# Float32 feature matmuls of 128 tokens split into two of 64 on halves of TensorE's columns

## The chip, the core and the metric

The kernel runs on one core of a Trainium2 chip. The metric is the device time of one execution in microseconds (us), from the first to the last work of the core; lower is better. TensorE does matrix products in two instructions, a weight load (LDWEIGHTS, written PEld in the profile) that puts the stationary operand (`lhsT`) into the array and a MATMUL (written PE) that streams the moving operand (`rhs`) through it into PSUM. VectorE is DVE, ScalarE is ACT, GpSimd is POOL and SyncE, which issues most DMAs, is SP.

## What is computed

Three layers run one after the other on 4 sequences of 1088 tokens. The first is a linear attention with 4 heads of 32 dimensions, the second a gated feed-forward layer of width 1024 whose input is mixed with the token before, the third a gated MLP that mixes along the sequence with a 1088 x 1088 matrix. The change lies in the first, in `phi`:

```python
def phi(x):
    a = np.einsum('rd,bhsd->bhsr', S1, x)
    b = np.einsum('rd,bhsd->bhsr', S2, x)
    return np.einsum('bhsi,bhsj->bhsij', a, b).reshape(*x.shape[:-1], r * r)
q_p, k_p = (phi(q), phi(k))
kv = np.einsum('bhsf,bhsd->bhfd', k_p, v)
z = np.sum(k_p, axis=2)
num = np.einsum('bhsf,bhfd->bhsd', q_p, kv)
den = np.einsum('bhsf,bhf->bhs', q_p, z)[..., None] + 1e-06
return (num / den).astype(np.float32)
```

With r = 8 each token and head gets 8 values `a` and 8 values `b`, that is 16 per head and 64 for the four heads, and their outer product of 64 features per head.

## The kernel before, in words

Queries and keys lie in SBUF with their 128 dimensions (4 heads x 32) on the partitions and the tokens along the free axis. A sequence of 1088 tokens is cut into three chunks of 384, 384 and 320 tokens (`CH`, line 22), so there are 12 chunks of queries and 12 of keys. `features` (line 204) handles one chunk: for each of its three blocks of 128 tokens (the last block of a 320-token chunk overlaps the one before) it issues one float32 matmul at line 208. Its weights are the 128 tokens (128 dimensions x 128 tokens), its moving operand is `Sbd`, a 128 x 128 matrix. The first 64 columns of `Sbd` are S1 and S2 laid out block by block for the four heads; the last 64 are zeros, since the mask `mk` that it is multiplied with (line 849) has ones only in its first four of eight columns. So a matmul writes 128 tokens on the PSUM partitions and 128 columns, of which the first 64 are wanted; the next block's matmul starts 64 columns further on and writes over the zeros. Each float32 matmul of the program becomes two passes on TensorE, each of one weight load and one MATMUL; 24 chunks with three blocks are 72 matmuls of the program and 144 passes in the trace.

After the three blocks ScalarE copies half of the 64 columns, or all of them, out of PSUM (line 211 or 216, through `copy` at line 134), and VectorE or GpSimd makes the outer product (line 219). For keys (`k_feat`, line 224) the features are summed with the values in `k_sum` (matmuls at line 239, mask at line 244). For queries (`q_feat`, line 249) they are transposed on TensorE (`q_turn`, line 260), multiplied with the sums (`q_num`, line 276, with the division at lines 280 to 282), and transposed back (`q_out`, line 294).

The feed-forward layer works on groups of 128 hidden features: `up` and `down` (lines 354 and 398) use three products of split operands in the faster float32r format (`mm3`, line 128, all under line 131) or one float32 product (line 406). The third layer, `spatial` and `group` (lines 548 and 694), fills the second half of the time with float32r products under line 131.

The order is set in three ways. The program first does the keys of sequence 0, the first chunk of queries, and the keys of sequence 1 (lines 892 to 931). Then one loop over the 96 groups of the feed-forward layer (line 1011) calls whatever `plan` has put down for a group: chunk j of queries at group `QS[j]`, its transposes, products and output two or three groups later, the keys of sequences 2 and 3 some groups ahead of their first query (lines 946 to 962). `behind` (line 896) holds single steps back until a named instruction has been issued. Last, the framework orders each engine's instructions by a simulated timeline (line 1157), so that the six passes of one chunk can stand apart on TensorE with other matmuls between them.

Of the kernel before, what the change touches and what calls it, by code (L numbers as in the profile page):

```python
# [21 lines left out]
CH = ((0, 384), (384, 384), (768, 320))  # L22
# [62 lines left out]
def attn_moe_gmlp(ctx: ExitStack, tc: tile.TileContext, qT, kT, va, st, wk, wv, wr, win, wout,  # L85
                  wT, wtail, btail, mu, ident, msk, out):
    nc = tc.nc
    TE, VE, SE, GE = nc.tensor, nc.vector, nc.scalar, nc.gpsimd
# [7 lines left out]
    def sb(tag, shape, dt=F32):  # L96
        uid[0] += 1
        return pool.tile(shape, dt, tag=tag, bufs=1, name=f"{tag}_{uid[0]}")

    def bank(i):  # L100
        uid[0] += 1
        return pp.tile([128, 512], F32, tag=f"p{i}", bufs=1, name=f"p{i}_{uid[0]}")
# [3 lines left out]
    def rot(*tags):  # L106
        i = count.get(tags, 0)
        count[tags] = i + 1
        return tags[i % len(tags)]

    def m(i):
        return f"m{i}"
# [20 lines left out]
    def copy(dst, src):  # L133
        return SE.activation(out=dst, in_=src, func=AF.Copy)  # L134
# [25 lines left out]
    def flat(r):  # L160
        return r.rearrange("p a b -> p (a b)")
# [14 lines left out]
    def cut(c, t, o=0):  # L176
        a = CH[c][1] - 128 if t == 2 else 128 * t
        return slice(o + a, o + a + 128)
# [25 lines left out]
    def features(src, c, dst, pb=4, eng=None, early=False):  # L204
        wide = bank(pb)
        ab = wide[:, :192].rearrange("p (t h r) -> p t h r", t=3, h=NH)
        for t in range(3):
            TE.matmul(wide[:, 64 * t:64 * t + 128], lhsT=src[:, cut(c, t, CH[c][0])], rhs=Sbd, start=True, stop=True)  # L208
        if eng is None:
            bs = sb(rot("bs0", "bs1"), [128, 3, NH, 8])  # L210
            copy(bs, ab[:, :, :, 8:16])
            a_ = ab[:, :, :, 0:8].rearrange("p t h i -> p (t h) i")
            b_ = bs.rearrange("p t h j -> p (t h) j")
        else:
            sab = sb(m(2 + c) if early else "sab", [128, 3, NH, 16])
            copy(sab, ab)
            a_ = sab[:, :, :, 0:8].rearrange("p t h i -> p (t h) i")
            b_ = sab[:, :, :, 8:16].rearrange("p t h j -> p (t h) j")
        outer[0] = (eng or VE).tensor_tensor(
            out=dst.rearrange("p t (h i j) -> p (t h) i j", h=NH, i=8),  # L220
            in0=a_.unsqueeze(3).to_broadcast([128, 3 * NH, 8, 8]),
            in1=b_.unsqueeze(2).to_broadcast([128, 3 * NH, 8, 8]), op=ALU.mult)

    def k_feat(b, c, pb=4, eng=None):
        kp = kps[b, c] = sb((KB1 if b == 1 else ("n0H", "n0L", "n1H"))[c], [128, 3, 256])
        features(k_s[b], c, kp, pb, GE if 3 * b + c in KP else eng, eng is not None)
# [22 lines left out]
    def q_feat(i):  # L249
        qp = qst[i] = sb("n1L", [128, 3, 256])  # L250
        features(q_s[i // 3], i % 3, qp, 4, GE if i in QP else None)
# [599 lines left out]
    Sbd = flat(Sb)  # L851
# [309 lines left out]
```

## Time and profile before

| what | value |
|---|---|
| median of 3 runs | 451.74 us |
| lowest and highest run | 451.67 and 452.97 us |
| span of the profiled execution, first to last instruction | 450.7 us |
| TensorE MATMUL busy | 440.8 us, 98% of the span, 2691 instructions |
| TensorE weight loads busy | 420.4 us, 93% |
| VectorE, ScalarE, GpSimd busy | 297.5, 270.4, 223.2 us |
| MATMULs of line 208 | 144, first start at 4.7 us, last at 130.2 us |

The profile gives the span of one execution from its first to its last instruction. It has no time of its own for that execution beside the span; the median run is 1.04 us longer than the span, and that is taken for what lies around it. MATMULs are pipelined: each record lasts from its issue to a modelled end, and the next one starts long before that end, so a MATMUL's duration isn't what it costs in a stream. The cost in a stream is the distance from one start, or end, to the next, which the chain of work that ended last shows: there each instruction counts only from the end of the one before it. "x6" after a piece is the number of instructions in it.

### The profile page before, as it was taken

What the parts mean: (1) busy time and instruction counts of PE and PEld (TensorE: products, weight loads), DVE (VectorE), ACT (ScalarE), POOL (GpSimd) and SP (SyncE); (2) the same over time, 40 slices, a digit from 0 to 9 for tenths busy, and PEclk for the clock granted to TensorE, in tenths of its full rate; (3) what the DMA queues carried; (4) which work ended last, traced back from release to release, by engine and by line L of the source; (5) the groups of instructions that cost most, each with busy time, mean ns of one, the idle gap of its engine ahead of it and who ended that gap; (6) DMA issues with size and microseconds to landing.
All of it is one profiled execution on the core that took longest, in us unless ns stands there. A gap on an engine that the chain in (4) does not pass through costs nothing.

```text
span 450.7 us, 7621 instructions
## 1 busy us (share of the span) xinstructions
PE 440.8 (98%) x2691; PEld 420.4 (93%) x2691; DVE 297.5 (66%) x531; ACT 270.4 (60%) x629; POOL 223.2 (50%) x271
## 2 busy tenths in 40 slices
PE   8899999999999999999999999999999999999997
PEld 7897989989998988899999999999999999999996
DVE  5995777779864986566587797862755951734513
ACT  2595888998977898767446664334545434533322
POOL 2166477496744585868222426544435534335220
PEclk9999999999999999999999999999999999999999
DMA  7981100011100030033238422313022232010001
GB/s 232 369 297 49 51 0 2 2 52 54 27 2 0 22 120 19 19 87 113 59 117 256 131 63 93 118 54 110 15 85 93 72 110 69 19 41 25 0 2 49
DMA packets 30950, 34.92 MB, mean 77 GB/s; under 512 B 2816, under 2 KB 26432, under 8 KB 30912
## 3 DMA queue, kind: packets, MB, share of 16 engines
q1 hardware_dynamic: 30768, 34.43, 23.8%
q8 instruction: 21, 0.34, 0.3%
q14 instruction: 17, 0.14, 0.1%
q10 hardware_dynamic: 144, 0.01, 0.0%
HBM read 25.91 MB, written 8.52 MB: 76 GB/s over the span
## 4 chain that ended last, share of the span: by engine, by line
PE 84%; DVE 6%; DMA 3%; ACT 3%; POOL 1%; issue 1%; SPq 1%; ACTq 0%; DVEq 0%
PE p L131 67%; PE p L406 5%; PE p L276 3%; PE p L239 2%; PE p L208 2%; DMA w<-in_wk_dram 1%; PE p L260 1%; PE p L722 1%; PE p L721 1%; DMA st<-in_wT_dram 1%; DVE w L148 1%; DVE w L147 1%; PE p L294 1%; ACT m L362 1%; DVE mx L319 1%
## 5 line engine op out<-in xcount | busy, mean ns | idle before, releaser
L131 PE MATMUL p<-m,k 128*128 128x384 f32 (+1 forms) x288 | 65.5, 349 | 0.0
L131 PE MATMUL p<-w,k 128*128 128x384 f32 (+1 forms) x360 | 63.8, 323 | 0.0
L131 PEld LDWEIGHTS p<-w,k 128*128 128x128 f32 x360 | 59.2, 188 | 0.3
L621 DVE TENSOR_TENSOR m<-p,m 128x384 f32<-128x384 f32 (+2 forms) x37 | 18.6, 520 | 57.0 <-PE p L722 56.1
L134 ACT ACTIVATE m<-m 128x384 fp32r<-128x384 f32 (+2 forms) x49 | 24.6, 502 | 45.9 <-DVE m L735 25.6
L131 PEld LDWEIGHTS p<-m,k 128*128 128x128 f32 x288 | 48.2, 189 | 4.1
L137 POOL TENSOR_TENSOR k<-VR,k 128x512 fp32r<-128x512 f32 x25 | 34.0, 1364 | 33.4 <-ACT k L134 28.6
L362 ACT ACTIVATE m<-p 128x384 f32<-128x384 f32 (+1 forms) x96 | 43.1, 468 | 8.2 <-PE p L131 6.4
L137 DVE TENSOR_TENSOR m<-m,m 128x384 fp32r<-128x384 f32 (+1 forms) x48 | 34.3, 715 | 11.2 <-ACT m L134 8.8
L131 PE MATMUL p<-w,n1H 128*128 128x384 f32 (+1 forms) x192 | 41.1, 326 | 0.0
L365 POOL TENSOR_TENSOR m<-m 128x384 f32<-128x384 f32 (+1 forms) x35 | 30.0, 859 | 21.5 <-ACT m L362 21.0
L137 DVE TENSOR_TENSOR w<-m,w 128x384 fp32r<-128x384 f32 (+1 forms) x35 | 26.0, 746 | 15.4 <-POOL m L365 11.4
L131 PE MATMUL p<-w,n1L 128*128 128x384 f32 (+1 forms) x168 | 34.8, 324 | 0.9 <-POOL n1L L137 0.9
L134 ACT ACTIVATE m<-p 128x384 f32<-128x384 f32 (+1 forms) x36 | 17.1, 482 | 30.0 <-PE p L131 21.7
L137 POOL TENSOR_TENSOR n1H<-VR,n1H 128x512 fp32r<-128x512 f32 x12 | 15.5, 1293 | 37.1 <-ACT n1H L134 26.4
L406 PE MATMUL p<-w,wvT 128*128 128x384 f32 (+1 forms) x86 | 33.4, 470 | 0.0
L131 PEld LDWEIGHTS p<-w,n1H 128*128 128x128 f32 x192 | 32.6, 188 | 0.5
L500 POOL TENSOR_SCALAR rs<-mv 128x1 f32<-128x1 f32 x34 | 8.8, 260 | 43.3 <-DVE mv L499 42.4
L131 PEld LDWEIGHTS p<-w,n1L 128*128 128x128 f32 x168 | 28.5, 188 | 1.4 <-POOL n1L L137 1.2
L504 DVE TENSOR_SCALAR VR<-VR,mv,rs 128x512 f32<-128x512 f32 x24 | 20.5, 855 | 12.6 <-POOL rs L501 12.3
L134 ACT ACTIVATE k<-VR 128x512 fp32r<-128x512 f32 x25 | 15.7, 630 | 21.4 <-PE p L131 17.1
L131 PE MATMUL p<-w,xs1H 128*128 128x384 f32 (+1 forms) x90 | 26.9, 338 | 0.0
(288 smaller groups left out, 1212.6 us busy)
## 6 DMA issues: line engine op xcount, KB each, us to landing
vd<-VR SPq DMA_DIRECT2D x24, 256.0 KB, 2.0
VR<-vd SPq DMA_DIRECT2D x24, 256.0 KB, 2.9
st<-in_wT_dram SPq DMA_DIRECT2D x16, 192.0 KB, 2.4
w<-in_kT_dram SPq DMA_DIRECT2D x8, 192.0 KB, 4.4
w<-in_qT_dram SPq DMA_DIRECT2D x8, 192.0 KB, 4.0
VR<-in_wT_dram SPq DMA_DIRECT2D x8, 192.0 KB, 2.6
out_dram<-m SPq DMA_DIRECT2D x8, 192.0 KB, 2.1
m<-in_wT_dram SPq DMA_DIRECT2D x8, 192.0 KB, 4.5
```

The costliest lines, as they stand in the source:

```text
L131: TE.matmul(out_ap, lhsT=l, rhs=r, start=first and n == 0, stop=last and n == 2, skip_group_check=skip)
L134: return SE.activation(out=dst, in_=src, func=AF.Copy)
L137: return eng.tensor_tensor(out=L, in0=src, in1=H.bitcast(F32), op=ALU.subtract)
L208: TE.matmul(wide[:, 64 * t:64 * t + 128], lhsT=src[:, cut(c, t, CH[c][0])], rhs=Sbd, start=True, stop=True)
L239: TE.matmul(kv[:, w * g:w * g + w], lhsT=kp, rhs=vt if wide else vt[:, VP * g:VP * g + VP], start=(t == 0), stop=(t == NT - 1))
L276: nd_pe[0] = TE.matmul(o.rearrange("p h c -> p (h c)"), lhsT=qt[g][:, cut(c, t)], rhs=kb[:, g], start=not wide or g == 0, stop=not wide or ...
L362: SE.activation(out=r, in_=hk, func=AF.Relu)
L365: anchor[2] = GE.tensor_tensor(out=sq, in0=r, in1=r, op=ALU.mult)
L406: TE.matmul(vvs[i], lhsT=wvT[:, f // 2], rhs=hls.pop(g), start=f == 0, stop=f == NF - 1)
L500: GE.tensor_scalar(out=rs, in0=mv[:, 1:2], scalar1=1e-6, scalar2=None, op0=ALU.add)
L504: VE.tensor_scalar(out=v, in0=r, scalar1=mv[:, 0:1], scalar2=rs, op0=ALU.subtract, op1=ALU.mult)
L621: return eng.tensor_tensor(out=o, in0=a, in1=b_, op=op)
```

## The change

Each matmul at line 208 becomes two. The weights of each are 64 of the 128 tokens, the moving operand is the first 64 columns of `Sbd`, and the result goes to PSUM partitions 0 to 63 for the first half and 64 to 127 for the second, into the 64 wanted columns only. A matmul with 64 columns of weights and an output that starts at partition 0 or 64 is placed on one half of the array's columns, over all 128 of its rows. Nothing else is touched: the copies, the outer products, the DMAs and the order of the calls are as they were. The zeros are no longer written, nor read by anything.

```diff
         for t in range(3):
-            TE.matmul(wide[:, 64 * t:64 * t + 128], lhsT=src[:, cut(c, t, CH[c][0])], rhs=Sbd, start=True, stop=True)
+            a = cut(c, t, CH[c][0]).start
+            for o in (0, 64):
+                TE.matmul(wide[o:o + 64, 64 * t:64 * t + 64], lhsT=src[:, a + o:a + o + 64], rhs=Sbd[:, :64], start=True, stop=True)
```

## Rows read from the trace of the kernel before

**Rows 1.** The page: busy time of each engine, and the granted TensorE clock in 40 slices.
```profile
PE 440.8 (98%) x2691; PEld 420.4 (93%) x2691; DVE 297.5 (66%) x531; ACT 270.4 (60%) x629; POOL 223.2 (50%) x271
...
PEclk9999999999999999999999999999999999999999
```

**Rows 2.** Stretches: start:end, length, each engine's busy us (x instructions), clock, DMA share, GB/s.
```profile
core 0: us, PE busy (x) PEld busy (x) DVE busy (x) ACT busy (x) POOL busy (x), PEclk, DMA share, GB/s
4.00:25.00 21.00, 19.14 (x153) 18.29 (x153) 17.05 (x31) 9.38 (x23) 1.51 (x2) 1.00 1.00 344
25.00:45.00 20.00, 18.91 (x128) 16.59 (x128) 15.12 (x28) 14.77 (x38) 14.87 (x13) 1.00 0.45 149
45.00:131.00 86.00, 85.33 (x542) 77.97 (x541) 67.23 (x116) 74.54 (x185) 55.99 (x60) 1.00 0.08 25
```

**Rows 3.** Line 208 alone in the same stretches: busy us (x passes), clock, DMA share, GB/s.
```profile
core 0: us, PE busy (x) PEld busy (x), PEclk, DMA share, GB/s
4.00:25.00 21.00, 6.37 (x48) 6.12 (x48) 1.00 1.00 344
25.00:45.00 20.00, 4.26 (x30) 3.88 (x30) 1.00 0.45 149
45.00:131.00 86.00, 9.94 (x66) 9.43 (x66) 1.00 0.08 25
```

**Rows 4.** The page: shares of the span on the chain that ended last.
```profile
PE 84%; DVE 6%; DMA 3%; ACT 3%; POOL 1%; issue 1%; SPq 1%; ACTq 0%; DVEq 0%
PE p L131 67%; PE p L406 5%; PE p L276 3%; PE p L239 2%; PE p L208 2%; DMA w<-in_wk_dram 1%; PE p L260 1%; PE p L722 1%; PE p L721 1%; DMA st<-in_wT_dram 1%; DVE w L148 1%; DVE w L147 1%; PE p L294 1%; ACT m L362 1%; DVE mx L319 1%
```

**Rows 5.** The same chain in order of time: start, length (us), what, how many.
```profile
4.48 6.67 DMA w<-in_wk_dram
...
17.42 0.57 DVE VR L282
...
33.75 0.67 PE p L208 x6
...
35.27 0.65 PE p L406 x2
...
45.61 1.29 PE p L276 x12
...
57.28 0.83 POOL mx L318
...
58.14 1.85 DVE mx L319
...
89.43 0.22 PE p L208 x2
...
129.82 0.67 PE p L208 x6
```

**Rows 6.** What TensorE waited for, first from 4 to 45 us, then from 45 to 160 us.
```profile
PE p L276 <- DVE kb L244: 1.1, 1, 1.1
PE p L294 <- DVE VR L282: 0.7, 2, 0.4
...
PE p L131 <- DVE de L281: 0.7, 1, 0.7
PE p L260 <- POOL n1L L219: 0.3, 1, 0.3
```

**Rows 7.** The timeline of PE from 33 to 47 us: start, length, instruction, tiles, shape.
```profile
33.58 0.83 PE L208 MATMUL p<-Sbd,w 128*128 128x128 f32 x6
...
35.11 0.81 PE L406 MATMUL p<-w,wvT 128*128 128x384 f32 x2
...
45.45 1.45 PE L276 MATMUL p<-kb,VR 128*128 128x66 f32 x12
```

**Rows 8.** Line 208, all its passes: duration ns min/median/max, first and last start, shape.
```profile
L208 PEld LDWEIGHTS p<-Sbd,w x144: 186/192/330, 4.4 to 130.1; 128*128 128x128 f32 x144
L208 PE MATMUL p<-Sbd,w x144: 270/275/377, 4.7 to 130.2; 128*128 128x128 f32 x144
```

**Rows 9.** Line 208 from 7.40 to 7.46 us, the one pass there, behind an idle TensorE.
```profile
L208 PEld LDWEIGHTS p<-Sbd,w x1: 186/186/186, 7.4 to 7.4; 128*128 128x128 f32 x1
L208 PE MATMUL p<-Sbd,w x1: 377/377/377, 7.4 to 7.4; 128*128 128x128 f32 x1
its engine sat idle before it (us, times) until:
  DMA w<-in_qT_dram: 1.2, 2
```

## The prediction

> **What bounds the kernel now.** I read the page first. TensorE is busy for 98% of the span at a granted clock of full speed in every slice, that is at the higher of its two levels, 2.4 GHz; no other engine passes 66% [rows 1]. But a share over the span hides stages, so the stretches come next, with line 208 alone in each. From 45 to 131 us TensorE is busy for 85.3 of 86.0 us, and 66 of the 144 passes of line 208 lie there; 30 lie between 25 and 45 us, and 48 before 25 us, where the DMA engines are full (share 1.00) [rows 2, 3]. Third is the chain of work that ended last: 84% of it is TensorE, and line 208 has 2% [rows 4]. Followed in time, it holds 17 pieces of line 208 from 33.75 to 129.82 us, nine of six passes, one of four and seven of two: 72 passes, exactly half of the 144, or 12 of the 24 chunks [rows 5]. The other half is beside something. Up to 25 us the chain runs over the load of `wk` and then VectorE, down to the division at 17.42 us [rows 5], and TensorE waits for VectorE for 1.1 and 0.7 us in all [rows 6]: the eight chunks (48 passes) before 25 us are covered by that. Of the five between 25 and 45 us three stand on the chain; of the eleven after 45 us nine do, and the other two lie beside GpSimd and VectorE around 57 us [rows 5]. The last view is the waits after 45 us: TensorE waits for 0.7 us and 0.3 us, no more [rows 6]. So on these 72 passes, each nanosecond more or less on TensorE is a nanosecond of the end.
>
> **What a pass costs now.** A MATMUL's record is 275 ns long [rows 8] but they overlap; on the chain six passes take 0.67 us, so 112 ns each, and 224 ns for one matmul of the program [rows 5]. Two other rows tell what makes the 112. A float32 pass with 384 moving columns takes 0.65/2 = 325 ns [rows 5, 7], so each further column costs (325 - 112)/256 = 0.83 ns and the part that doesn't depend on columns is 112 - 128 x 0.83 = 5.5 ns. A pass with only 66 moving columns, but the same 128 columns of weights, still takes 1.29/12 = 107.5 ns [rows 5, 7]; its columns would need 60 ns. So the weight load, or the issue of the pair, has a floor of its own at 107.5 ns, and in line 208 that floor and the moving columns weigh the same. The zeros in the moving operand are thus nearly free: dropping them alone would save 4.5 ns a pass.
>
> **What the change adds and removes.** 72 matmuls of the program become 144, so 144 passes become 288: weights half as wide, moving columns halved. No DMA is issued and no wait is added; the copy that reads the bank waits for the last of twelve passes in place of six, and behind it nothing else is queued that TensorE needs at once (the next matmuls are of the feed-forward layer). I cost that copy's delay at nothing while TensorE has such work; without it the delay is the lengthening of one burst, below.
>
> *One pass.* The moving columns give 64 x 0.83 + 5.5 = 59 ns. The weight floor is seen at one width only. Bounds: if it falls with the width, 107.5/2 = 54 ns; if it is issue and doesn't fall, 107.5 ns. I take 59, since a 66-column pass is 4.5 ns cheaper than a 128-column one and a weight load's record of 192 ns [rows 8] is long enough to be streaming. One after the other, twelve passes take 708 ns where six took 672: +36 ns a chunk, 12 x 36 = **+0.4 us**. At 107.5 ns they take 1290 ns: +618 ns a chunk, +7.4 us.
>
> *Two halves side by side.* The halves use different columns of the array and write different partitions. If the second half's first pass runs beside the first half's second pass, and so on down the burst, two passes go in each slot of 59 ns: 6 x 59 = 354 ns, -318 ns a chunk, **-3.8 us**. No row shows two MATMULs of this kernel side by side: every piece above is in single file. I take zero as the nearest row, and keep -3.8 us as the bound.
>
> *The change of shape.* The passes of before have weights of 128 x 128, one after another [rows 7]. After the change TensorE goes from full width to half and back around each of the 17 pieces on the chain, 34 times. No row shows such a step. Below: nothing, since weight loads now run ahead of the MATMUL before them whatever its line. Middle: the new weights can't be loaded ahead, as in the pass behind an idle TensorE at 7.44 us, whose MATMUL starts with its load and takes 377 ns where the median is 275, 102 ns more [rows 8, 9]. That is 102 ns on the way back and, with half the columns, 51 on the way in: 153 ns a piece, 17 x 153 = **+2.6 us**. Above: TensorE also empties first, so that 275 - 112 = 163 ns of each last pass is bare; 34 x 163 = 5.5 us more, +8.1 us. I take the middle, because it is the one row in which a load wasn't hidden. The 12 chunks off the chain would take 12 x 36 ns and at most 12 x 153 ns, 2.3 us; these lie under the load of `wk` and VectorE early on, and if that cover were gone these 2.3 us came on top.
>
> The sum: +0.4 + 2.6 = **+3.0 us** on a span of 450.7 us, that is 453.7 us; with the 1.04 us by which the median run exceeds the span, **454.7 us** against 451.74, 0.7% slower.
>
> A rule that bears on the last term: the Trainium skill, page "TensorEngine Tiling (Array Packing)", section "Key Properties", says that changing the tiling mode, not just the tile, drains TensorE. By that rule the step is at its upper bound, and the time would be 460.2 us; no run here shows it yet.
>
> **Rivals.**
>
> *Side by side, and the change of shape is free.* -3.8 us, 447.9 us. For it: the two halves share neither columns nor PSUM partitions, and loads already run under MATMULs here. Against it: the two halves read their weights in turn, and a floor of 107.5 ns for a pass with few columns says that loads are a stream of their own; if they stay in single file at 54 ns each, twelve take 648 ns and nothing is won. The place is the 17 pieces; it decides as soon as the overlap saves a chunk more than 2.6/12 us = 217 ns. The same page, same section, says that different tiles can load weights and multiply in parallel; no row here shows that.
>
> *Side by side, with the loads bare at each step.* -3.8 + 2.6 = -1.2 us, 450.5 us: within 0.3% of before, which is about what a measurement of this kernel can tell from no change (1.36 us).
>
> *In single file and the step free*, so the change of shape and the parallel halves both don't exist: +0.4 us, 452.1 us. This is also what is seen if the halves are run as ordinary full-width matmuls with idle columns.
>
> *TensorE empties at each step.* +0.4 + 8.1 = 460.2 us in single file, 456.0 us side by side. For it: every one of the 17 pieces stands alone among matmuls of full width. Against it: in the present trace a line never costs extra behind another one, but these all have one shape.
>
> *The order changes.* The framework places 12 matmuls where 6 stood and may part them more often; seven pieces of two passes are there already. Each further piece on the chain costs 153 ns by the middle price, ten of them 1.5 us.
>
> **How the numbers follow.** Forecast (single file, loads bare) 0.33; side by side and free 0.20; side by side with bare loads 0.17, a third of that beyond the 0.3%; single file and free 0.15; emptying 0.10; another order or a floor of issue 0.05. Faster by over 0.3%: 0.20 + 0.05 + 0.02 = 0.27. Within: 0.12 + 0.15 + 0.02 = 0.29. Slower: 0.33 + 0.10 + 0.01 = 0.44. The range goes from the side-by-side case less a little, 447.4 us, to 459.0 us, which leaves out emptying in single file and a floor of issue for all passes. The forecast's own range is 453 to 457 us, by further pieces or a dearer step.
>
> **What would show it.** Right: 288 passes under the changed line, about 59 ns from one to the next in a burst, and the next matmul of full width some 100 ns later than behind a pass of before. Side by side: bursts of twelve that take about 0.35 us on the chain, where six took 0.67. Emptying: gaps of 160 ns or more ahead of and behind each burst. Wrong altogether: pieces of unchanged total length, or a difference that lies outside 25 to 131 us.

## The result and the profile after

The changed kernel takes 457.01 us (median of 4 runs, 456.36 to 457.19) where the kernel before takes 452.29 us (4 runs): a ratio of 1.0097, 95% interval 1.0080 to 1.0113. It is slower, by 4.7 us; the span of the profiled execution went from 450.7 to 455.4 us, also 4.7 us.

All passes of the feature matmuls (now line 210; the lines below it have moved by two), durations in ns as min/median/max, and the longest entry of what ended the idle time ahead of them:
```profile
L210 PEld LDWEIGHTS p<-Sbd,w x288: 132/138/227, 4.7 to 139.4; 128*64 128x64 f32 x144
L210 PE MATMUL p<-Sbd,w x288: 222/222/320, 4.7 to 139.5; 128*64 128x64 f32 x144
...
its engine sat idle before it (us, times) until:
  issue: 5.3, 22
```

These answer to [rows 8]: 288 passes of half the width. New is the last line: 22 times the record of the weight loads (PEld) is empty just ahead of such a pass, for 5.3 us in all, and the cause is "issue", that is nothing that the profile shows: no semaphore, no other engine. The same view of the kernel before names a DMA (1.2 us, twice) and ScalarE (0.3 us, once) there, and no "issue". The record of the MATMULs has no such hole, since theirs overlap.

One chunk kept together, the timeline of PE and of its weight loads from 55.7 to 57.1 us (start, length, instruction, count):
```profile
55.69 0.51 PE L131 MATMUL p<-w,xs1H 128*128 128x384 f32 x2
56.13 0.57 PE L210 MATMUL p<-Sbd,w 128*64 128x64 f32 x12
56.62 0.80 PE L131 MATMUL p<-m,k 128*128 128x384 f32 x3
...
56.12 0.43 PEld L210 LDWEIGHTS p<-Sbd,w 128*64 128x64 f32 x12 [0.25 <-issue]
```
And the first 40 ns of it, line 210 from 56.10 to 56.14 us:
```profile
L210 PE MATMUL p<-Sbd,w x2: 270/270/270, 56.1 to 56.1; 128*64 128x64 f32 x2
```

Read in four steps. **Side by side:** twelve passes have their first and last start within 0.57 - 0.22 = 0.35 us (five steps of 58 ns and the 0.05 us of the next step), and two of them start in the first 40 ns, while a half that runs alone, further down, has its two passes 0.33 - 0.22 = 0.11 us apart. So the halves do run beside each other: six slots of 58 ns in place of six passes of 112. **Way in:** the MATMUL ahead started at 55.86 us (the second of the two at 55.69, each 0.17 us); behind it one of full width would have started 0.17 us later, this one starts at 56.13, after 0.27: 0.09 us in which nothing starts. I read them as TensorE emptying; the trace shows the gap and not its cause. Its first two passes last 270 ns where the median is 222: 0.05 us of bare weight load. **Way out:** the last pass starts at 56.70 - 0.22 = 56.48 us (56.474 unrounded), the next matmul of full width at 56.62 (56.625), after 0.15 where a slot is 0.058: 0.09 us of emptying; and that one lasts 441 ns where 338 is usual, 0.10 us of bare load. **Together** 0.09 + 0.05 + 0.09 + 0.10, some 0.35 us, once for each piece, however many passes it has. (With some narrower matmuls behind it the same reckoning gives 0.30.) From the end of the MATMUL ahead (56.20) to the end of the first one behind (57.42 less two more of 0.175) are 0.87 us; less that one's own 0.175 the piece cost 0.70 us. Six passes of before cost 0.67 [rows 5]. A chunk that stays together is thus nearly even. One that is broken up is not:
```profile
89.57 0.38 PE L262 MATMUL p<-idn,n1L 128*128 128x128 f32 x2
89.88 0.33 PE L210 MATMUL p<-Sbd,w 128*64 128x64 f32 x2
90.14 0.79 PE L131 MATMUL p<-m,k 128*128 128x384 f32 x3
```
By the same reckoning (90.93 - 0.35 - 89.95 - 0.175) this single half of a block, without a partner, costs 0.46 us. Two passes of before, which did a whole block, cost 0.22 [rows 5].

The framework made many such pieces. From 27 us on there are 29 (before: 21): seven of 12 passes, three of ten, one of eight, seven of six, three of four and eight of two. An odd half runs alone, so these 192 passes take 114 slots in place of 96. The sum is 29 x 0.35 + 114 x 0.058 = 16.7 us against 96 x 0.112 = 10.8 us. Reckoned from the trace for each of the 29 pieces by itself, as for the two above, it is 16.1 us against 10.7, the waits left out: **+5.4 us on TensorE**. What TensorE waited for from 27 to 215 us (in total, times, longest):
```profile
PE p L131 <- DVE w L137: 0.8, 1, 0.8
PE p L131 <- DVE de L283: 0.8, 1, 0.8
PE p L131 <- ACT w L396: 0.7, 1, 0.7
PE p L262 <- DVE n1L L221: 0.2, 1, 0.2
```
That is 2.5 us; the same view of the kernel before has 3.3 us (0.9 and 0.3 for GpSimd, 0.7 for ScalarE, 0.7, 0.4 and 0.3 for VectorE). A slower TensorE waits 0.8 us less: 5.4 - 0.8 = 4.6 us after 27 us. That looks like the whole of the 4.7 us, but it isn't quite, for something is lost earlier as well. The first division on VectorE, which starts at 17.42 us in [rows 5], starts here at
```profile
18.23 0.56 DVE L284 TENSOR_TENSOR VR<-p,de 128x384 f32<-128x384 f32 x1
```
0.8 us later, and what TensorE does behind it is as late. Early and late together come to 5.4 us, 0.7 more than the span shows; the view of the waits leaves out the shortest, and these 0.7 us stay unaccounted for.

### The profile page after: what moved, and what is told of

It is laid out like the page before. It is cut to its first block, busy times and chain, and to the rows that moved or that the text cites. A ratio compares the mean times of both kernels' runs of the same rounds, so it can differ in the third digit from the quotient of the medians.

```text
span 455.4 us, 7909 instructions
## 1 busy us (share of the span) xinstructions
PE 445.4 (98%) x2835; PEld 417.3 (92%) x2835; DVE 296.7 (65%) x531; ACT 270.5 (59%) x629; POOL 221.9 (49%) x271
## 4 chain that ended last, share of the span: by engine, by line
PE 46%; DVE 3%; ACT 2%; DMA 2%; issue 1%; POOL 0%; ACTq 0%; SPq 0%
PE p L131 43%; PE p L724 1%; PE p L723 1%; DMA vd<-VR 1%; DVE m L623 1%; DMA VR<-vd 1%; DMA st<-in_wT_dram 1%; DVE VR L623 1%; ACT m L134 1%; DVE VR L506 0%; DVE m L137 0%; DVE xs0L L137 0%; DVE bn L500 0%; ACT T L134 0%; POOL rs L503 0%
## 5 line engine op out<-in xcount | busy, mean ns | idle before, releaser
L137 DVE TENSOR_TENSOR w<-m,w 128x384 fp32r<-128x384 f32 (+1 forms) x35 | 24.6, 708 | 16.9 <-ACT w L396 6.1
```

Of the source, the lines that this page charges most:

```text
L137: return eng.tensor_tensor(out=L, in0=src, in1=H.bitcast(F32), op=ALU.subtract)
```

## Experiments

Kernels that ran on the same chip share the runs of the kernel before (medians 452.0 to 452.4 us). Ratios are to it, with the 95% interval; times of kernels from different chips are best compared by their distance to it.

### Pieces kept together, and its control

In the changed kernel the first matmul of a chunk stays where it is, and the other five are queued right behind it with priority; the control does the same to the three of the kernel before. Both have 20 pieces, 16 of them after 27 us.
```diff
+        lead = None
         for t in range(3):
             a = cut(c, t, CH[c][0]).start
             for o in (0, 64):
-                TE.matmul(...)
+                with ExitStack() as es:
+                    if lead is not None:
+                        es.enter_context(tc.issue_after(lead.ins))
+                        es.enter_context(tc.high_priority())
+                    x = TE.matmul(...)
+                    lead = lead or x
```


> The changed kernel, but the twelve passes of a chunk are kept together on TensorE (20 pieces in place of 33). Theory A (the loss is a fixed price of each change of shape, about 0.35 us for a piece however many passes it has, while the passes themselves run two at a time in 58 ns): from 27 us on there are 16 pieces in place of 29, so 13 x 0.35 = 4.5 us and some 1.0 us of half matmuls that found no partner go away; of these 5.5 us a fifth was beside other work, so about 4.4 us: 452 to 453 us, level with the kernel before. Theory B (the halves themselves are slow, or the new order of the other matmuls costs the time): still 456 to 457 us.

> The kernel before, with the three matmuls of a chunk kept together in the same way (20 pieces in place of 25), no change of shape. Theory A: at full width a piece has no price, so nothing changes: 451.5 to 453 us. If keeping them together is itself worth or costs something, it shows here and must be taken off the run above.

Measured: 454.46 us (1.0048, 1.0032 to 1.0065), and the control 452.75 us (1.0014, 1.0002 to 1.0027). The breaking up is over half of the loss: 457.0 to 454.5 us. Theory A had 452 to 453 us, and the miss is the last 1.7 us above the control. TensorE's own sum is 16 x 0.35 + 96 x 0.058 = 11.1 us, +0.4 us on before, so it isn't there. Its waits from 27 to 215 us in this run add up to 4.0 us, 0.7 more than before and 1.2 more than in the control (2.8), among them new ones on operands that other engines make for the feed-forward layer:
```profile
PE p L131 <- ACT xrH L134: 0.8, 2, 0.4
PE p L131 <- DVE x L418: 0.5, 1, 0.5
PE p L131 <- POOL xrL L137: 0.5, 1, 0.5
```
0.4 + 1.2 = 1.6 us of the 1.8 us by which the spans of this run and the control differ (452.4 and 450.6). So theory A holds for the pieces, and the rest is waits. The framework lays the order of the other engines' work anew for every program; that these waits come from that order is likely but not shown.

### Narrow passes without halves

Full width, two matmuls of 32 wanted columns in place of one, each chunk kept together as above (the lines for that are left out, here and in the next section).
```diff
         for t in range(3):
-            TE.matmul(wide[:, 64 * t:64 * t + 128], lhsT=src[:, cut(c, t, CH[c][0])], rhs=Sbd, ...)
+            for o in (0, 32):
+                TE.matmul(wide[:, 64 * t + o:64 * t + o + 32], lhsT=src[:, cut(c, t, CH[c][0])], rhs=Sbd[:, o:o + 32], ...)
```


> Full width kept, pieces kept together, but each matmul becomes two of 128 tokens with 32 of the 64 wanted columns each: 288 passes without any change of shape and without halves of the array. Theory A (a pass of full width has a floor of 107.5 ns that is its weight load): twelve passes take 1290 ns, +618 ns a chunk, +7 us or more: 459 to 462 us. Rival (the cost falls with the moving columns, so the gain of halves is only that of narrow passes): about as before, 452 to 453 us, and passes under 60 ns apart.

Measured: 466.51 us (1.0310, 1.0292 to 1.0327). One chunk, timeline of PE from 51.7 us:
```profile
52.07 1.42 PE L214 MATMUL p<-Sbd,w 128*128 128x32 f32 x12
53.33 0.86 PE L283 MATMUL p<-kb,VR 128*128 128x66 f32 x6
```
Twelve passes with 32 columns take 53.33 - 52.07 = 1.26 us, 105 ns each: a quarter of the columns of before saves 7 ns of 112. The floor is real and belongs to the full-width weights; only half-width weights get under it. The loss is 14 us and not 7, because the early chunks, too, had come out from under their cover: the first division starts at 21.92 us in place of 17.42, so 4.5 us were lost by then, in part at the lower clock (granted 0.50 from 9 to 16 us). That 24 chunks x 0.58 us would be 13.8 us proves nothing, as it leaves out the clock and the waits.

### Lower halves first, then upper halves

```diff
-        for t in range(3):
-            for o in (0, 64):
+        for o in (0, 64):
+            for t in range(3):
```


> The changed kernel with pieces kept together, but the three lower halves first and then the three upper halves. Theory A (TensorE runs two passes side by side only if passes for the other half of the columns stand next to it in its queue): ten of twelve passes in single file, about 11 slots of 58 ns in place of 6, +0.29 us a chunk, on 12 to 16 chunks +3.5 to +4.6 us over the run with pieces kept together: 456 to 457 us. Rival (each half draws its own passes from anywhere in the queue): no change against that run, starts still in pairs 7 ns apart.

Measured: 454.07 us (1.0034, 1.0022 to 1.0046). A chunk, timeline of PE:
```profile
51.84 0.77 PE L131 MATMUL p<-m,k 128*128 128x384 f32 x3
52.54 0.73 PE L215 MATMUL p<-Sbd,w 128*64 128x64 f32 x12
```
From first to last start are 0.73 - 0.22 = 0.51 us: neither six slots (0.35) nor twelve in single file (11 x 0.058 + 0.05 = 0.69). The upper half's passes begin 0.17 us after the lower half's, three passes late, and then run beside the rest. So in this burst TensorE doesn't need partners next to each other, but it doesn't look the whole queue ahead either: theory A is wrong by 2 us in the time, its rival wrong in the starts. The 0.16 us a chunk don't show in the time, which is level with the run above within the intervals: on TensorE they are 16 x 0.16 = 2.6 us, and TensorE's waits from 27 to 215 us are 1.8 us fewer than in that run (2.2 for 4.0). So work on TensorE at these places need not lengthen the run: it can take the place of a wait.

### One more parting in each chunk, and its control

A matmul of full width into columns that nobody reads, between the second and the third block; in the control the same in the kernel before, kept together.
```diff
+                if t == 1 and o:
+                    with ExitStack() as es:
+                        es.enter_context(tc.issue_after(lead.ins))
+                        es.enter_context(tc.high_priority())
+                        TE.matmul(wide[:, 256:384], lhsT=src[:, cut(c, t, CH[c][0])], rhs=Sbd, start=True, stop=True)
```


> The changed kernel with pieces kept together, and in each chunk one more matmul of full width (128 tokens, 128 columns, into columns of the bank that nobody reads) between the second and the third block, so that each piece is parted in two. Theory A (a piece has a fixed price of 0.35 us): per chunk 224 ns of own passes + 0.35 us, on 12 to 16 chunks +6.9 to +9.1 us over the run with pieces kept together (454.5 us): 461 to 464 us. Rival (a change of shape is free): only the passes, +2.7 to +3.6 us: 457 to 458 us.

> The kernel before with its three matmuls kept together and the same additional matmul of full width behind the second block: no change of shape. Both theories: 224 ns a chunk on 12 to 16 chunks, +2.7 to +3.6 us: 455.4 to 456.4 us. The difference of the run above to this one, less that of the two kernels without the additional matmul (454.5 and 452.75 us), is the price of one more parting alone: 4.2 to 5.6 us by theory A, 0 by the rival.

Measured: 460.22 us (1.0196, 1.0151 to 1.0241) and 455.48 us (1.0072, 1.0055 to 1.0088). The parted piece, timeline of PE:
```profile
54.68 0.45 PE L215 MATMUL p<-Sbd,w 128*64 128x64 f32 x8
55.06 0.49 PE L221 MATMUL p<-Sbd,w 128*128 128x128 f32 x2
55.48 0.34 PE L215 MATMUL p<-Sbd,w 128*64 128x64 f32 x4
55.75 0.62 PE L131 MATMUL p<-m,k 128*128 128x384 f32 x2
```
From 54.68 to the next matmul at 55.75 are 1.07 us; the unparted piece above takes 56.62 - 56.13 = 0.49. Less 0.22 for the two full passes, one parting costs 0.36 us. In all 16 pieces of the trace together it is 5.4 us. In the time: (460.22 - 455.48) - (454.46 - 452.75) = 3.0 us. One of the four runs took 464.4 us, which makes this difference uncertain by some 2 us; it is over zero, and with the trace the rival falls, but its middle is below the 4.2 to 5.6 us of theory A, and the parted kernel is faster than the 461 to 464 us expected. The trace says where the rest is. TensorE's waits from 27 to 215 us, 4.0 us in the kernel with unparted pieces, are here
```profile
PE p L131 <- POOL n1L L137: 0.8, 1, 0.8
PE p L131 <- ACT n1H L134: 0.3, 1, 0.3
PE p L419 <- ACT m L395: 0.3, 1, 0.3
```
1.4 us, while those of the two kernels of full width are about alike (2.5 and 2.8 us): 5.4 - 2.6 = 2.8 us. The price is right; that each part of it reaches the end is not.

### The wanted columns alone

```diff
-            TE.matmul(wide[:, 64 * t:64 * t + 128], lhsT=src[:, cut(c, t, CH[c][0])], rhs=Sbd, start=True, stop=True)
+            TE.matmul(wide[:, 64 * t:64 * t + 64], lhsT=src[:, cut(c, t, CH[c][0])], rhs=Sbd[:, :64], start=True, stop=True)
```


> One part of the change alone: 128 tokens at full width, but only the 64 wanted columns. By the prediction's floor of 107.5 ns a pass, 72 passes on the chain save 4.5 ns each: -0.3 us, not to be told from no change: 451.5 to 453 us. Rival (narrow passes are the gain that the halves bring): six passes in 0.35 us, about -3.8 us: 448.5 us.

Measured: 454.78 us (1.0052, 1.0033 to 1.0070), slower, which neither expected. The chain of the first microseconds (start, length, what), then line 208 from 5 to 14 us:
```profile
4.87 5.01 PE p L208 x24
```
```profile
L208 PEld LDWEIGHTS p<-Sbd,w x23: 331/333/334, 4.7 to 9.4; 128*128 128x128 f32 x23
L208 PE MATMUL p<-Sbd,w x23: 420/421/422, 4.8 to 9.5; 128*128 128x64 f32 x23
```
The first 24 passes take 209 ns each, twice the 105 ns of a narrow pass of full width above, and their weight loads 333 ns where 192 is usual [rows 8]: TensorE was at the lower of its two levels, 1.2 GHz. The trace's list of granted clocks has its first entry, of full speed, only at 14.1 us, though the engine was busy throughout; in the kernel before that entry stands at 4.9 us. (A stretch ahead of the first entry is printed as 1.00: the mean clock of this execution reads 1.000.) The first division starts 2.6 us later than in [rows 5]:
```profile
20.03 0.56 DVE L282 TENSOR_TENSOR VR<-p,de 128x384 f32<-128x384 f32 x1
```
The next run keeps the zeros for the first seven chunks (the line that sets `narrow[0]` behind them is left out).
```diff
+            n = 64 if narrow[0] else 128
-            TE.matmul(wide[:, 64 * t:64 * t + 128], lhsT=src[:, cut(c, t, CH[c][0])], rhs=Sbd, start=True, stop=True)
+            TE.matmul(wide[:, 64 * t:64 * t + n], lhsT=src[:, cut(c, t, CH[c][0])], rhs=Sbd[:, :n], start=True, stop=True)
```


> Full width with only the 64 wanted columns, but the first seven chunks with the zeros as before. In the run without any zeros (454.8 us) the passes up to 14 us ran at the lower clock, and 2.6 us of its loss were there by 18 us. If that clock is the cause: 451.5 to 453 us. Rival (passes of 64 columns at full width are dearer in the stretch where TensorE is the bound): still 454 us or more.

Measured: 453.05 us (1.0023, 1.0011 to 1.0034), just above the 451.5 to 453 us expected. The first division is back where it was:
```profile
17.51 0.56 DVE L285 TENSOR_TENSOR VR<-p,de 128x384 f32<-128x384 f32 x1
```
So the early zeros had a use: with them the clock rose early, the first entry of full speed standing at 6.9 us. Measured from the kernel before on the same chip, the loss falls from 2.4 to 1.0 us; the remaining 0.2% I can't tell from another order of the work.

In the changed kernel the clock is at most a small part. Its profiled execution falls to the lower level for a while, after TensorE had sat idle twice around 6 to 8 us (stretches as in [rows 2]):
```profile
4.00:8.00 4.00, 2.30 (x41) 1.65 (x42) 2.48 (x4) 0.75 (x3) 0.00 (x0) 1.00 0.94 247
8.00:11.50 3.50, 3.50 (x23) 3.38 (x24) 1.92 (x4) 0.43 (x2) 0.25 (x1) 0.51 0.99 353
```
and it is 0.8 us late at the first division, where the kept-together kernel, with halves as well but no such fall, is not (17.47 us). So the fall is the likely cause of these 0.8 us, though no run shows it by itself. Of its four runs two have a mean granted clock of 0.996 and two of 1.000, and their times overlap (457.15 and 456.88 us; 456.36 and 457.19 us). That doesn't clear the clock, as a mean of 1.000 can hide a late rise; it leaves the 4 us behind 27 us untouched.

### Chunks of keys and queries merged

If a piece has a fixed price, fewer and longer pieces should win. Each chunk of keys of sequences 2 and 3 goes into the same bank as a chunk of queries and is issued right with it; the sums follow one group later. The control is the same at full width.
```diff
+    def both(b, c, i):
+        wide = bank(4)
+        kp = kps[b, c] = sb(("n0H", "n0L", "n1H")[c], [128, 3, 256])
+        qp = qst[i] = sb("n1L", [128, 3, 256])
+        place(wide[:, :192], k_s[b], c)
+        place(wide[:, 192:384], q_s[i // 3], i % 3, True)
+        features(q_s[i // 3], i % 3, qp, 4, GE if i in QP else None, wide=wide[:, 192:384])
+        features(k_s[b], c, kp, 4, GE if 3 * b + c in KP else None, wide=wide[:, :192])
...
+    WITH = {3 * b - 2 + c: (b, c) for b in (2, 3) for c in range(3)}
...
-            plan(last + 1, k_sum, b, 0)
-            plan(last + 2, k_sum, b, 1)
+            plan(last + 2, k_sum, b, 0)
+            plan(last + 3, k_sum, b, 1)
```


> The changed kernel with pieces kept together, and each chunk of keys of sequences 2 and 3 placed in the same bank as, and issued right behind, a chunk of queries: six pieces of 24 passes in place of twelve of 12, 14 pieces in all. Theory A: six fixed prices of 0.35 us less, -2.1 us against the run with pieces kept together (454.5 us): 452 to 453 us, and 451 us if the waits after 160 us are as before. Rival (what is left of the loss in that run comes from the order of the other work): 454 us or more.

> The same merging of chunks of keys with chunks of queries (14 pieces), at full width with the matmuls of the kernel before: no change of shape. Theory A: a piece of full width has no price, so its number is worth nothing: 451.5 to 453 us, 2 to 3 us above the merged run with halves (449.8 us). Rival (the merging is worth something by another order of the work, and the halves nothing): 449 to 450.5 us.

Measured: **449.79 us** (0.9943, 0.9928 to 0.9958), faster than both kernels and 1 to 3 us below what theory A gave, and the control 453.76 us (1.0041, 1.0026 to 1.0056), 0.8 us above its range. Merging at full width loses 1.7 us, so of the 4.0 us between the two not all is the halves' gain; against the kernel before it is 2.6 us. A piece of the merged run, timeline of PE:
```profile
52.91 0.51 PE L131 MATMUL p<-w,xs1H 128*128 128x384 f32 x2
53.35 0.92 PE L216 MATMUL p<-Sbd,w 128*64 128x64 f32 x24
54.20 0.79 PE L131 MATMUL p<-m,k 128*128 128x384 f32 x3
```
By the reckoning from above (54.99 - 0.35 - 53.42 - 0.175) two chunks cost 1.05 us where before they cost 1.34. From 27 us on there are ten pieces, 10 x 0.35 + 96 x 0.058 = 9.1 us against 10.8: -1.7 us on TensorE, against the control as well. The rest is fewer waits, 2.3 us from 27 to 215 us against 3.3:
```profile
PE p L131 <- POOL m L137: 0.6, 1, 0.6
PE p L131 <- ACT m L376: 0.6, 1, 0.6
PE p L131 <- ACT m L387: 0.4, 1, 0.4
PE p L131 <- DVE m L137: 0.3, 1, 0.3
PE p L131 <- DVE m L395: 0.2, 1, 0.2
PE p L131 <- ACT bs L134: 0.2, 1, 0.2
```
-1.7 - 1.0 = -2.7 us; the span shows -2.2. The control waits for 3.7 us, so to it the two sums are -1.7 - 1.4 = -3.1 us, where the spans differ by 3.6 (452.1 and 448.5). How much of the shorter waits comes with the halves and how much with this order isn't settled.

One more run took the halves out of the first seven chunks of this kernel, which seemed to be covered (`halves[0] = True` stands behind those chunks).
```diff
+            for o in (0, 64) if halves[0] else (None,):
+                    if o is None:
+                        x = TE.matmul(wide[:, 64 * t:64 * t + 128], lhsT=src[:, a:a + 128], rhs=Sbd, start=True, stop=True)
...
+    halves[0] = True
```


> The merged kernel with halves, but the first seven chunks (keys of sequence 0, first queries, keys of sequence 1) at full width as in the kernel before. These lie under the load of the first weights and VectorE, so neither what halves save there nor their four fixed prices should be seen: 449 to 450.5 us. Rival (the early chunks count): a shift of 1 us or more, to either side.

Measured: 451.57 us (0.9986, 0.9974 to 0.9997), 1.8 us above the merged run. A miss: something of the early halves counts, or the order that follows from them does. The first division, in the merged kernel and in this one, starts at
```profile
17.83 0.56 DVE L307 TENSOR_TENSOR VR<-p,de 128x384 f32<-128x384 f32 x1
17.46 0.56 DVE L310 TENSOR_TENSOR VR<-p,de 128x384 f32<-128x384 f32 x1
```
so without the early halves the kernel is 0.4 us ahead there and loses it later. Behind 27 us both have ten pieces with halves, and TensorE waits for 3.0 us here and 2.3 there. So it isn't the time of the early chunks themselves, but what follows from the order; 0.7 us of it are these waits, the rest stays open.

## Why the prediction came out as it did

It said slower by 3.0 us, 454.7 us, within 447.4 to 459.0, and the time is 457.0 us, slower by 4.7. The direction and the range were right; the sum was right for reasons that are only partly so, since two of its choices failed and leaned against each other. With both put right on its 17 pieces and 12 chunks, it reads -3.8 + 17 x 0.35 = +2.2 us, close to its +3.0 by luck; the rest of the 4.7 us is the breaking up, which it left to a small chance, and the early 0.8 us, less the shorter waits.

- *What bounds the kernel:* right in the main. The work on TensorE and its waits make up the difference to within 0.7 us in the changed kernel and, each against its control, to within 0.2 us in the kept-together and 0.5 us in the merged one. But not each nanosecond on TensorE was a nanosecond of the end: 2.6 us more of it with the lower halves first cost no time, and of 5.4 us for one more parting some 3 reached the end. TensorE then waited less.
- *One pass, 59 ns:* right, a slot takes 58 ns. That the weight floor falls with the width was chosen rightly between the two bounds; at full width it stays (105 ns with 32 columns).
- *Two halves side by side:* wrong. I took zero, because no row showed two MATMULs abreast, and kept -318 ns a chunk as the bound. The bound was the truth: six slots, 350 ns in place of 672. The trace of before could not show this, as everything in it had one shape. The Trainium skill, page "TensorEngine Tiling (Array Packing)", section "Key Properties", says that different tiles can load weights and multiply in parallel, and the passes that start in the same 40 ns agree.
- *The change of shape:* the middle was taken, bare loads only. The loads came out as said, 0.05 + 0.10 us for 51 + 102 ns. But there are also 0.09 us on the way in and as much on the way out, which I read as TensorE emptying, where the upper bound had 0.163 each: 0.35 us a piece and not 0.153. The Trainium skill, same page and section, says that a change of tiling mode drains TensorE; the gaps of 0.09 us agree, at a little over half the price that I had worked out for it.
- *The number of pieces:* 17 on the chain were counted as they stood, and the rival of another order allowed for ten more at 153 ns. There are 29 after 27 us, and halves without partners on top. With the same passes kept together the kernel takes 454.5 us.
- *The rivals:* the case that happened is the small one of an engine that empties while the halves run side by side, 456.0 us, which shared a chance of 0.10. Single file is out, and so is a free step: a piece of 12 passes shows six slots and 0.35 us around them.
- *The cover of the early chunks* held in the kept-together kernels with halves (first division at 17.47 and 17.20 us, before at 17.42), but not as a rule: with passes of 105 ns, or at the lower clock, the chunks before 18 us came out from under it, and in the profiled execution of the changed kernel 0.8 us did.
- *The 1.04 us* added to the span joined the median to the span of another execution; where a run here has both numbers, the time is 1.7 to 1.9 us longer than its own span. The forecast difference of +3.0 us doesn't hang on it.

What I should have weighed more: a change of shape is paid for each piece, so the first question was how many passes a piece would have, and that is the framework's choice.

## What to carry to other kernels

In this kernel two halves of TensorE's columns came near to doubling the rate of narrow float32 matmuls (twelve passes in six slots of 58 ns for six of 112), but entering and leaving that shape cost some 0.35 us together, so a stay had to last longer than twelve passes to pay. So gather such matmuls into long unbroken runs, and look at the engine's actual order for how often it is parted, before counting the gain. A term for which the trace of before has no row of its kind should be settled by a small experiment; here two such terms were each misjudged by several microseconds, to opposite sides, and cancelled in part by luck.

## What the runs showed that was not expected

- Each half draws its passes by itself, within limits: with all lower halves queued ahead of the upper ones, the upper half still started three passes, 0.17 us, after the lower.
- Zeros that nobody reads were worth 1.4 us, measured from the kernel before on each chip: without them the first 24 passes ran at 1.2 GHz, 209 ns each, and the clock's first entry of full speed came at 14.1 in place of 4.9 us.
- The order that the framework lays for the same work moves the time by itself: the two controls at full width, which issue the same instructions as the kernel before in another order (one of them with two chunks to a bank), stand at 1.0014 (1.0002 to 1.0027) and 1.0041 (1.0026 to 1.0056).
- Work added to the engine that bounds the kernel can be free: with the lower halves first TensorE had 2.6 us more to do and waited 1.8 us less, and the time was the same within the intervals.
